# Re-ordered start, DMA transposes and new item weights in a planned adaLN block on one NeuronCore

## The chip, the cores and the metric

The kernel runs on one core of a Trainium2 chip. The metric is the device time of one launch in microseconds, taken as the median over runs. One more execution was taken by the hardware profiler, and all durations below come from that one.

## The reference

The input `x` has 2048 tokens of width 448. A condition row `c` gives six modulation rows by `silu(c) @ w_mod`. The block is an attention part and an MLP part, each behind a layer norm with modulation and each with a gated residual:

```python
sa, ca, ga, sb, cb, gb = (silu(c) @ w_mod) split in six
h = layernorm(x) * (1 + ca) + sa
x = x + ga * A(h)          # A: 16 heads of 28, each query sees 8 keys, 2 tokens apart; then @ wo
h = layernorm(x) * (1 + cb) + sb
x = x + gb * B(h)          # B: gelu(layernorm(h) @ w1 + b1) @ w2 + b2, inner width 1792
```

## The kernel before

**Tiling.** The tokens are held in two halves, the even tokens and then the odd ones, so that a window with steps of 2 becomes 8 neighbours within a half. There are 16 blocks of 128 tokens (`x_all`), and four chunks of 4 blocks. Attention runs in 17 groups (g0 to g16) of 121 queries against 128 keys.

**Stages.** The *front end* of a chunk takes the statistics of x (line 372), the power -1/2 on GpSimd (392), the normalised rows `z` in a `zbuf` (397), the transposes by TensorE into the PSUM tile `ptr` (482), and the modulation out of PSUM into `hT` (490 on ScalarE, 493 on VectorE). The projections to q and k follow (`pq`, 504), and their copies into `qT` and `kT` (360, 362). Chunk 0 is split into two front ends of two blocks, `front_end(0, 2, "x0")` and `front_end(2, 2, "x2")`; the others, of four blocks, begin at blocks 4, 8 and 12. *Attention* of a group is the logits `lt` (581), two exponentials `ex` (592), the mask `mk` (601), the values `pv` (616), `po` (626), the division `rd` and `on` (633, 637), a transpose `pt` (647) and its copy into `oT`. Per block follow the output projection `wo` (668) and the residual `x1` (673). The *second norm* (372 to 397, 692) ends in a `ybuf`, which a DMA issued by SyncE transposes into `yT` (707). The *MLP* of a chunk is `w1` (723) in 7 items of 8 matmuls, `ge`, the gelu (730), and per block `w2` (752), 14 matmuls. The term gb*b2 enters as one more matmul per block, ones-like `share` against the rows `gbb2_rows` (750). `fin` (762) adds the residual on VectorE, and SyncE stores the block (768).

**What sets the order.** Every step is an item of a `Plan` with the engines that it may run on and its duration on each. `Plan.order` simulates them once, at build time: among the items that are ready it picks the one with the earliest start, and among equal starts the longest remaining path, `tail`. `PRI` adds a weight to the tail of all items of a kind. Items are then emitted in the order of their simulated starts, so each engine's instruction order is fixed. `LANDS` gives the plan a time at which each load is there. `PHASES = [10, 17, 17, 17]` says how many attention groups come ahead of each chunk's MLP: the logits after a phase stand behind the last `w1` item of the MLP before, and its exponentials behind the last gelu. `SLOTS` counts the PSUM and SBUF buffers of each kind; `ptr`, `lt` and the output `p1` of w1 share the two buffers of the kind `lt`.

**The start.** SyncE issues the loads of c, of the first third of `w_mod` (`wmod`, columns sa and ca), of k, q and v weights and of the rest; ScalarE issues the loads x0 and x2. GpSimd clears pads and makes `ident` and `mask1`, VectorE copies `mask1` into `mask_rest` (560) and `silu_bf` into `silu_bc` (450). `idle(n)` issues n matmuls on zeros that nothing reads. 32 matmuls of one column (`ps_col`, 429) turn the modulation rows sa and ca into columns, which `mod1` (435 to 438) takes out of PSUM.

The key by which the plan before picks an item is

```python
key = (s, -tail[i], i)
```

Of the kernel before, what the change touches and what calls it, by code (L numbers as in the profile page):

```python
# [16 lines left out]
KT = 4  # L17
# [15 lines left out]
PHASES = [10, 17, 17, 17]  # L33
W2S = [(0, 5), (5, 10), (10, 14)]
SLOTS = {"lt": 2, "s": 3, "p2": 1, "et": 2, "on": 2, "vb": 3, "z2": 2, "yT": 2, "hm": 2, "xp": 4}

LANDS = [("c", 3.0), ("x0", 4.0), ("x2", 4.6), ("wmod", 7.8), ("wk", 8.6), ("wq", 9.4), ("wv", 10.3), ("x4", 12.5),
         ("wmod2", 18.0), ("wo", 19.5), ("b2", 20.5), ("x8", 22.0), ("w1", 28.0), ("w2", 33.0)]
NIDLE = 14
PLANS = None  # L40

PRI = {"po": -68.5, "r3": 10.0, "ve": -28.0, "lt": 6.0, "on": -24.0, "w2": -9.0, "ex": -20.0, "zt": 7.0,
       "r2": 53.3, "ge": -12.0, "w1": -13.0, "yt": 4.0, "y": 6.0, "z2": -7.0, "ml": -1.7, "pb": -5.0, "ot": 3.7,
       "pt": -0.6, "rd": 1.1, "h": 7.0, "mk": -2.0}
STATS_ACT = 2.0
XP = "PE"
# [5 lines left out]
class Plan:  # L52
# [8 lines left out]
    def add(self, name, eng, needs=(), after=(), uses=(), allocs=(), lag=0.09, tab=None, at=0.0, fn=None, pri=0.0):  # L61

        i = len(self.ops)
        self.index[name] = i
        self.ops.append(dict(name=name, eng=eng, needs=list(needs), after=list(after), allocs=list(allocs), lag=lag,
                             tab=tab, at=at, fn=fn, pri=pri + PRI.get(re.match(r"[a-z]+([0-9](?=_))?", name)[0], 0.0)))
        for b in list(uses) + list(allocs):
            self.bufs[b][1].append(i)

    def order(self, hop=0.07, table=1.3, win=3.413):  # L70
# [44 lines left out]
        while ready:  # L115
            best = None
            for i in ready:
                o = ops[i]
                t = o["at"]
                for j in o["need_i"]:  # L120
                    same = ops[j]["ran"] in o["eng"] and len(o["eng"]) == 1
                    t = max(t, end[j] + (0.0 if same else hop))
                for j in o["after_i"]:
                    t = max(t, start[j])
                ok, cntt = True, {}
                for b in o["allocs"]:
                    tg = tag_of[b]
                    st = slot_time(tg, cntt.get(tg, 0))
                    cntt[tg] = cntt.get(tg, 0) + 1
                    if st is None:  # L130
                        ok = False
                        break
                    t = max(t, st)
                if not ok:
                    continue
                fin = {e: max(t, free[e]) + d for e, d in o["eng"].items()}
                e = min(fin, key=lambda e: (fin[e], e))
                s = max(t, free[e])
                if o["tab"] and tab not in (None, o["tab"]):
                    s += table  # L140
                key = (s, -tail[i], i)
                if best is None or key < best[0]:
                    best = (key, i, e, s)
# [33 lines left out]
def kernel(  # L177
# [55 lines left out]
    NX1P = 4  # L233
    if XP == "PE":

        share = cst.tile([128, 128], BF16, name="share")
        gbb2_rows = cst.tile([128, D], BF16, name="gbb2_rows")
    else:
        x1p_ring = cst.tile([128, NX1P, D], FP32, name="x1p_ring")
# [18 lines left out]
    NZB = 3  # L258
# [17 lines left out]
    nc.sync.dma_start(out=c_row[:], in_=c)  # L276
    nc.scalar.dma_start(out=x_all[:, 0:2, :], in_=xv[:, 0, 0:2, :])
    nc.scalar.dma_start(out=x_all[:, 2:4, :], in_=xv[:, 0, 2:4, :])
    WM1 = 2 * D
    wmod = stp.tile([128, KT, WM1], BF16, name="wmod")  # L280
    load_ktiles(nc.sync, wmod, w_mod[:, 0:WM1], 0)
    wqk_st = stp.tile([128, KT, 2 * D], BF16, name="wqk_st")
# [19 lines left out]
    idle(4)  # L302
    for zb in zbufs:
        nc.vector.memset(zb[:, D:DP], 0.0)
    nc.gpsimd.memset(neg_half[:], -0.5)
# [5 lines left out]
    nc.gpsimd.memset(Wqk[64:128, KT - 1, :, :], 0.0)  # L311
# [3 lines left out]
    nc.gpsimd.memset(Wv[64:128, KT - 1, :], 0.0)  # L315
# [5 lines left out]
    nc.gpsimd.memset(wo_s[0:ZR_N, KT - 1, :], 0.0)  # L321
# [17 lines left out]
    if XP == "PE":  # L339
        nc.gpsimd.memset(share[:], 1.0 / 64)  # L340
# [7 lines left out]
    nc.gpsimd.memset(w1_s[64:128, KT - 1, :], 0.0)  # L348
# [74 lines left out]
    def col_fn(e):  # L423
        ps_col = T["ps_col"] = ps_s.tile([128, 2 * KT], FP32, name="ps_col", tag="s")
        for v in range(2):
            for j in range(KT):
                nj = kr_of(j)
                for kt in range(KT):
                    nc.tensor.matmul(ps_col[0:nj, v * KT + j:v * KT + j + 1],
                                     lhsT=wmod[0:kr_of(kt), kt, v * D + j * 128:v * D + j * 128 + nj],  # L430
                                     rhs=silu_bf[0:kr_of(kt), kt:kt + 1], start=(kt == 0), stop=(kt == KT - 1))
# [15 lines left out]
    P.add("idle", {"PE": 3.0}, after=["ps_c"], fn=lambda e: idle(NIDLE), pri=50.0)  # L447
    P.add("ps_col", {"PE": 1.3}, needs=["silu", "wmod"], after=["idle"], allocs=["ps_col"], lag=0.2, fn=col_fn)
    P.add("mod1", {"DVE": 0.3}, needs=["ps_col"], uses=["ps_col"], fn=mod1_fn)
    P.add("silu_bc", {"DVE": 0.33}, needs=["silu"], fn=lambda e: nc.vector.tensor_copy(  # L450
# [13 lines left out]
    def front_end(b0, nb, x_at):  # L464
        f = ("fe", b0)
        P.buf(f"ptr{b0}", "lt")
        for i in range(nb):
            stats(f"fst{b0 + i}", f, nb, i, lambda b=b0 + i: x_all[:, b, :], needs=[x_at])
        rstd(f"frs{b0}", f, nb, needs=[f"agfst{b0 + i}" for i in range(nb)])
        for i in range(nb):  # L470
# [6 lines left out]
            zs[zi] = b  # L477
            def t_fn(e, b=b, i=i, zi=zi):
# [8 lines left out]
        for kt in range(KT):  # L487
            def h_fn(e, kt=kt):
                if e == "ACT":
                    nc.scalar.activation(out=hT[:, kt, c0:c0 + w], in_=T["ptr", b0][:, kt, 0:w], func=ACT.Identity,  # L490
                                         bias=sa_col[:, kt:kt + 1], scale=ca1_col[:, kt:kt + 1])
                else:
                    nc.vector.tensor_scalar(out=hT[:, kt, c0:c0 + w], in0=T["ptr", b0][:, kt, 0:w],  # L493
                                            scalar1=ca1_col[:, kt:kt + 1], scalar2=sa_col[:, kt:kt + 1],
                                            op0=ALU.mult, op1=ALU.add)
            P.add(f"h{b0}.{kt}", {"ACT": 0.25 + 0.00084 * w, "DVE": 0.19 + 0.00053 * w},
                  needs=[f"zt{b0 + i}" for i in range(nb)] + ["mod1"], uses=[f"ptr{b0}"], fn=h_fn)
# [21 lines left out]
    for c4 in range(1, NCH):  # L519
        front_end(4 * c4, 4, "x4" if c4 == 1 else "x8")  # L520
# [20 lines left out]
    def use_gb(e, pb):  # L541
        nc.vector.tensor_copy(out=gb_bc[:], in_=pb[:])
        if XP == "PE":
            nc.vector.tensor_tensor(out=gbb2_rows[:], in0=pb[:], in1=b2_bc[:], op=ALU.mult)
            nc.vector.tensor_tensor(out=gbb2_bc[64:128, :], in0=pb[64:128, :], in1=b2_bc[64:128, :], op=ALU.mult)
            nc.vector.tensor_tensor(out=gbb2_rows[64:128, :], in0=gbb2_bc[64:128, :], in1=gbb2_rows[64:128, :],
                                    op=ALU.subtract)
        else:
            nc.vector.tensor_tensor(out=gbb2_bc[:], in0=pb[:], in1=b2_bc[:], op=ALU.mult)
# [10 lines left out]
    P.add("mask", {"DVE": 0.65}, fn=lambda e: nc.vector.tensor_copy(  # L560
# [151 lines left out]
    def mlp_items(c, gelu_after, w1_after):  # L712
# [23 lines left out]
        for bi, b in enumerate(bs):  # L736
            P.buf(f"p2_{b}", "s" if last and bi >= SLOTS["p2"] else "p2")
            if XP == "DVE":
                P.buf(f"xp{b}", "xp")
                def x_fn(e, b=b):  # L740
                    nc.vector.tensor_tensor(out=x1p_ring[:, b % NX1P, :], in0=x1_blk(b), in1=gbb2_bc[:], op=ALU.add)
                P.add(f"xp{b}", {"DVE": 0.53}, needs=[f"x1_{b}", "pb_gbe"], allocs=[f"xp{b}"],
                      after=[f"xp{b - 1}"] if b else [], fn=x_fn)
            for q in range(FT // 2):
                def fn(e, b=b, bi=bi, q=q):
                    if q == 0:
                        pool = ps_s if P.bufs[f"p2_{b}"][0] == "s" else ps_p2
                        T["p2", b] = pool.tile([128, D], FP32, name="p2", tag=P.bufs[f"p2_{b}"][0])
                        if XP == "PE":
                            nc.tensor.matmul(T["p2", b][:], lhsT=share[:], rhs=gbb2_rows[:], start=True, stop=False)  # L750
                    for ft in (2 * q, 2 * q + 1):
                        nc.tensor.matmul(T["p2", b][:], lhsT=T["hm", c][:, ft, bi * 128:(bi + 1) * 128],  # L752
                                         rhs=w2_s[:, ft, :], start=(ft == 0 and XP != "PE"), stop=(ft == FT - 1))
                kw = dict(uses=[f"hm{c}", f"p2_{b}"]) if q else dict(uses=[f"hm{c}"], allocs=[f"p2_{b}"])
                ws = [f"w2s{i}" for i, (f0, f1) in enumerate(W2S) if f0 < 2 * q + 2 and f1 > 2 * q]
                if XP == "PE" and q == 0:
                    ws = ws + ["pb_gbe"]
                P.add(f"w2_{b}.{q}", {"PE": (3 if XP == "PE" and q == 0 else 2) * 448 / 2400 + 0.005},
                      needs=[f"ge{c}.{q}"] + ws, lag=0.17, fn=fn,
                      after=[f"w2_{b}.{q - 1}"] if q else [], **kw)  # L760
            def f_fn(e, b=b):
                nc.vector.tensor_tensor(out=x_all[:, b, :], in0=T["p2", b][:], in1=x1_blk(b) if XP == "PE" else x1p_ring[:, b % NX1P, :],  # L762
                                        op=ALU.add)
            P.add(f"fin{b}", {"DVE": 0.54}, needs=[f"w2_{b}.{FT // 2 - 1}"] + ([f"xp{b}"] if XP != "PE" else []),
                  uses=[f"p2_{b}"] + ([f"xp{b}"] if XP != "PE" else []),
                  fn=f_fn)
# [22 lines left out]
    open_items = {P.index[n] for n in ("ps_col", "silu", "c_col", "wk0", "wk1", "wq0", "wq1", "ps_c", "idle")}  # L789
# [41 lines left out]
```

## Time and profile before

| What | Value |
|---|---|
| Median of 3 runs | 199.88 us (199.66 to 200.58) |
| The profiled execution's own time | 199.31 us |
| Its span, first to last instruction | 197.6 us |
| TensorE busy | 184.9 us, 1488 matmuls |
| VectorE, ScalarE, GpSimd busy | 129.8, 104.4, 24.8 us |
| Mean granted TensorE clock | 0.98 |
| Moved by DMA | 13.36 MB, nearly all in the first 30 us |

The span is what the instructions cover; the time of the execution is 1.7 us longer. A busy TensorE counts a matmul from its start to its modelled end, and matmuls overlap, so the pitch of a long run of them says more than their duration.

### The profile page before, as it was taken

How to read it: one execution, taken by the hardware profiler on the slowest of the kernel's cores; microseconds unless marked ns; L12 is line 12 of the kernel's file. 1: busy time of each engine (PE TensorE's matmuls, PEld its weight loads, DVE VectorE, ACT ScalarE, POOL GpSimd, SP SyncE). 2: the span in 40 equal slices, each digit the busy share in tenths (PEclk: the TensorE clock that was granted, in tenths of full speed). 3: DMA queues.
4: the chain of work that ended last, by engine and by line, in shares of the span. 5: the costliest groups of instructions: out<-in, count | busy, mean ns of one | idle time of the engine just before them, and what ended most of it. 6: DMA issues, size and time to landing. Idle time of an engine off the chain costs nothing.

```text
span 197.6 us, 3714 instructions
## 1 busy us (share of the span) xinstructions
PE 184.9 (94%) x1488; PEld 98.1 (50%) x1502; DVE 129.8 (66%) x325; ACT 104.4 (53%) x146; POOL 24.8 (13%) x57
## 2 busy tenths in 40 slices
PE   7949969989899999999989999999999999999993
PEld 2537745556454554545445555544444445444451
DVE  1877689989798799899879999899711011120021
ACT  3434879683888788465858665744224620204420
POOL 8732001100010201102000101211200000000000
PEclk9975999999999999999999999999999999999998
DMA  5999990000002020000230000015240000000002
GB/s 186 314 388 325 347 299 8 0 0 5 0 3 53 0 52 6 3 0 0 53 79 24 3 23 3 2 27 105 61 95 23 0 23 27 23 23 25 0 3 93
DMA packets 18454, 13.36 MB, mean 68 GB/s; under 512 B 9282, under 2 KB 17539, under 8 KB 18436
## 3 DMA queue, kind: packets, MB, share of 16 engines
q1 hardware_dynamic: 17892, 12.66, 22.1%
q10 hardware_dynamic: 544, 0.46, 0.8%
q8 instruction: 12, 0.20, 0.4%
q14 instruction: 6, 0.05, 0.1%
HBM read 9.18 MB, written 1.84 MB: 56 GB/s over the span
## 4 chain that ended last, share of the span: by engine, by line
PE 71%; DVE 17%; POOL 4%; ACT 3%; issue 3%; DMA 1%; POOLq 0%
PE p L752 20%; PE p L723 17%; PE pq L504 14%; PE pv L616 5%; PE pw L668 4%; DVE st L372 3%; ACT hT L490 3%; PE lt L581 2%; PE po L626 2%; DVE hT L493 2%; PE pt L647 2%; PE p L750 2%; POOL rs L392 2%; DVE x_all L673 2%; PE ptr L482 1%
## 5 line engine op out<-in xcount | busy, mean ns | idle before, releaser
L730 ACT ACTIVATE hm<-p 128x1024 bf16<-128x1024 f32 x28 | 28.6, 1024 | 52.1 <-PE p L723 51.0
L723 PE MATMUL p<-yT,w_s 128*128 128x512 bf16 x215 | 51.0, 379 | 0.6 <-DMA yT<-ybuf 0.2
L752 PE MATMUL p<-w_s,hm 128*128 128x448 bf16 x224 | 47.1, 352 | 0.0
L762 DVE TENSOR_TENSOR x_all<-p,x_all 128x448 bf16<-128x448 f32 x16 | 9.8, 620 | 46.0 <-PE p L752 46.0
L592 ACT ACTIVATE et<-lt 128x1024 bf16<-128x1024 f32 x34 | 33.7, 1030 | 5.5 <-PE lt L581 5.5
L723 PEld LDWEIGHTS <-w_s 128*128 128x128 bf16 x224 | 21.5, 98 | 24.9 <-issue 0.8
L504 PE MATMUL pq<-hT,Wqk 128*128 128x512 bf16 (+1 forms) x155 | 31.8, 355 | 0.9 <-DVE hT L493 0.5
L392 POOL TENSOR_TENSOR rs<-tv,neg_half 128x2 f32<-128x2 f32 (+1 forms) x21 | 17.1, 818 | 116.5 <-DVE tv L389 115.4
L752 PEld LDWEIGHTS <-hm 128*128 128x128 bf16 x224 | 21.3, 98 | 20.3 <-issue 1.0
L504 PEld LDWEIGHTS <-Wqk 128*128 128x128 bf16 x160 | 16.0, 105 | 12.3 <-issue 0.8
L601 DVE TENSOR_TENSOR et<-et,mask_rest 128x2048 bf16<-128x2048 bf16 x17 | 20.5, 1207 | 0.1
L372 DVE BATCH_NORM_STATS2 st<-x_all 128x6 f32<-128x448 bf16 x31 | 18.3, 609 | 0.1
L616 PE MATMUL pv<-Wv,hT 128*128 128x448 bf16 x68 | 15.3, 353 | 0.3 <-ACT kT L362 0.3
L668 PE MATMUL pw<-wo_s,oT 128*128 128x448 bf16 x64 | 14.6, 353 | 0.1
L362 ACT CAST vbuf<-pv 128x448 bf16<-128x448 f32 x15 | 8.1, 538 | 7.3 <-PE pv L616 7.2
L362 ACT CAST qT<-pq 128x512 bf16<-128x512 f32 (+1 forms) x19 | 9.5, 509 | 3.1 <-PE pq L504 2.8
L673 DVE TENSOR_TENSOR x_all<-pw,x_all 128x448 bf16<-128x448 f32 x16 | 9.9, 619 | 1.8 <-PE pw L668 1.8
L626 PEld LDWEIGHTS <-et 128*128 128x128 bf16 x272 | 9.0, 96 | 3.2 <-DVE vbuf L360 0.8
L637 DVE TENSOR_TENSOR on<-po,rden 128x448 bf16<-128x448 f32 x17 | 10.4, 614 | 0.1
L362 ACT CAST kT<-pq 128x512 bf16<-128x512 f32 (+1 forms) x17 | 8.5, 504 | 3.3 <-PE pq L504 3.0
L626 PE MATMUL po<-vbuf,et 128*128 128x29 bf16 x272 | 9.3, 176 | 0.5 <-DVE vbuf L360 0.5
L490 ACT ACTIVATE hT<-ptr,sa_col,ca_col 128x512 bf16<-128x512 bf16 (+1 forms) x10 | 6.7, 716 | 5.5 <-DVE hT L493 4.7
(99 smaller groups left out, 170.1 us busy)
## 6 DMA issues: line engine op xcount, KB each, us to landing
out_dram<-x_all SPq DMA_DIRECT2D x16, 112.0 KB, 1.7
w_s<-in_B_w_dram SPq DMA_DIRECT2D x1, 1568.0 KB, 13.9
wmod<-in_w_mod_dram SPq DMA_DIRECT2D x1, 1344.0 KB
w_s<-in_B_w_dram SPq DMA_DIRECT2D x1, 1344.0 KB, 14.9
x_all<-in_A_x_dram SPq DMA_DIRECT2D x1, 896.0 KB
wmod<-in_w_mod_dram SPq DMA_DIRECT2D x1, 672.0 KB, 5.3
wqk_st<-in_A_wqkv_dram SPq DMA_DIRECT2D x2, 336.0 KB, 5.8
x_all<-in_A_x_dram ACTq DMA_DIRECT2D x2, 224.0 KB, 4.1
```

The lines of the kernel that those rows point to most:

```text
L362: nc.scalar.copy(out=out, in_=in_)
L372: nc.vector.bn_stats(out=st[:], in_=src())
L392: nc.gpsimd.tensor_tensor(out=rs[:], in0=T["tv", tile_key][:], in1=neg_half[:, 0:n], op=ALU.pow)
L504: nc.tensor.matmul(pq[:, 0:w], lhsT=Wqk[:, kt, m, :], rhs=hT[:, kt, c0:c0 + w], start=(kt == 0), stop=(kt == KT - 1))
L592: nc.scalar.activation(out=et_v[:, 2 * half:2 * half + 2], in_=T["lt", g][half][:].rearrange("p r (ft c) -> p r ft c", ft=4), func=ACT.Exp ...
L601: nc.vector.tensor_tensor(out=et[:], in0=et[:], in1=mask_rest[:], op=ALU.mult)
L616: nc.tensor.matmul(pv[:], lhsT=hT[:, kt, k0:k0 + BK], rhs=Wv[:, kt, :], start=(kt == 0), stop=(kt == KT - 1))
L626: nc.tensor.matmul(po[:, h, :], lhsT=T["et", g][:, h, :], rhs=vbufs[g % NVB][:, h, :], start=True, stop=True)
L668: nc.tensor.matmul(pw[:], lhsT=oT[:, kt, jb * 128:(jb + 1) * 128], rhs=wo_s[:, kt, :], start=(kt == 0), stop=(kt == KT - 1))
L723: nc.tensor.matmul(p1[:, f, 0:w], lhsT=w1_s[:, kt, ft * 128:(ft + 1) * 128], rhs=T["yT", c][:, kt, 0:w], start=(kt == 0), stop=(kt == KT - 1))
L730: nc.scalar.activation(out=T["hm", c][:, 2 * q:2 * q + 2, 0:w], in_=T["p1", c, q][:, :, 0:w], func=ACT.Gelu_apprx_tanh)
L752: nc.tensor.matmul(T["p2", b][:], lhsT=T["hm", c][:, ft, bi * 128:(bi + 1) * 128], rhs=w2_s[:, ft, :], start=(ft == 0 and XP != "PE"), sto ...
```

## The change

- **Loads.** `wmod` is split into the columns sa (on SyncE's queue) and ca (on ScalarE's queue, behind x0 and ahead of x2). The plan gets their times as `wmsa` and `wmca`.
- **Start.** Four clears move from GpSimd to VectorE. `silu_bc` and `mask` may not start in the plan before 10.0 us (`later`). `ps_col` becomes two items, `ps_sa` and `ps_ca`. 11 idle matmuls stand where 14 stood, and 4 more after `ps_ca` and `zt1`. The statistics of blocks 2 and 3 stand behind `frs0a`.
- **Transposes.** For the chunks at blocks 8 and 12 (`Z_DMA`), `z` is transposed by a DMA of SyncE straight into `hT`, and the modulation runs in place in `hT`, on VectorE alone. A fourth `zbuf` is added.
- **gb*b2.** The extra matmul stays for blocks 0 to 3 and 15 (`XPE`). For the other 11, `fin` is two additions on VectorE, the first with `gbb2_bc` into an fp32 tile `xt`.
- **Order.** `PHASES` becomes `[9, 14, 17, 17]`. The key weighs the tail against the start (`LOOK`), `PRI` has new values, and `NUDGE` adds weights to about 140 single items.

```diff
-PHASES = [10, 17, 17, 17]
+PHASES = [9, 14, 17, 17]
...
-LANDS = [("c", 3.0), ("x0", 4.0), ("x2", 4.6), ("wmod", 7.8), ("wk", 8.6), ("wq", 9.4), ("wv", 10.3), ("x4", 12.5),
-         ("wmod2", 18.0), ("wo", 19.5), ("b2", 20.5), ("x8", 22.0), ("w1", 28.0), ("w2", 33.0)]
-NIDLE = 14
+LANDS = [("c", 3.0), ("x0", 5.0), ("x2", 5.8), ("wmsa", 6.4), ("wmca", 7.2), ("wk", 8.4), ("wq", 9.4), ("later", 10.0),
+         ("wv", 10.4), ("x4", 12.5), ("wmod2", 18.0), ("wo", 19.5), ("b2", 20.5), ("x8", 22.0), ("w1", 28.0),
+         ("w2", 33.0)]
+NIDLE = [11, 4]
+LOOK = 0.000121
+PRI = {"ad": -181.5, "agfst": -82.1, "ags2": -347.3, "ex": -137.9, "ge": -154.4, "h": -94.5, "lt": 209.3,
...
+NUDGE = {"ad12": 15.6, "ad2": -30.3, "ad8": 44.8, "agfst12": -48.8, "agfst6": 98.9, "ags2_13": -79.7,
...
-XP = "PE"
+Z_DMA = (2, 3)
+XPE = (0, 1, 2, 3, 15)
...
-                key = (s, -tail[i], i)
+                key = (s - LOOK * tail[i], -tail[i], i)
...
     nc.scalar.dma_start(out=x_all[:, 0:2, :], in_=xv[:, 0, 0:2, :])
+    load_ktiles(nc.sync, wmod[:, :, 0, :], w_mod[:, 0:D], 0)
+    load_ktiles(nc.scalar, wmod[:, :, 1, :], w_mod[:, D:2 * D], 0)
     nc.scalar.dma_start(out=x_all[:, 2:4, :], in_=xv[:, 0, 2:4, :])
-    load_ktiles(nc.sync, wmod, w_mod[:, 0:WM1], 0)
...
+    nc.vector.memset(Wqk[64:128, KT - 1, :, :], 0.0)
     for zb in zbufs:
         nc.vector.memset(zb[:, D:DP], 0.0)
+    nc.vector.memset(Wv[64:128, KT - 1, :], 0.0)
+    nc.vector.memset(wo_s[0:ZR_N, KT - 1, :], 0.0)
+    nc.vector.memset(w1_s[64:128, KT - 1, :], 0.0)
...
-    P.add("idle", {"PE": 3.0}, after=["ps_c"], fn=lambda e: idle(NIDLE), pri=50.0)
+    P.add("idle", {"PE": 2.4}, after=["ps_c"], fn=lambda e: idle(NIDLE[0]), pri=50.0)
+    P.add("ps_sa", {"PE": 1.05}, needs=["silu", "wmsa"], after=["idle"], allocs=["ps_col"], lag=0.2,
+          fn=lambda e: col_fn(0), pri=20.0)
+    P.add("ps_ca", {"PE": 1.05}, needs=["ps_sa", "wmca"], uses=["ps_col"], lag=0.2, fn=lambda e: col_fn(1), pri=20.0)
+    P.add("idle2", {"PE": 0.213 * NIDLE[1]}, after=["ps_ca", "zt1"], fn=lambda e: idle(NIDLE[1]), pri=50.0)
...
+            if by_dma:
+                P.add(f"zt{b}", {"SP": 1.25}, needs=[f"z{b}"], after=[f"zt{b - 1}"] if i else [], lag=1.2,
+                      fn=lambda e, b=b, zi=zi: nc.sync.dma_start_transpose(
+                          out=hT[:, :, tok_col(b):tok_col(b) + 128], in_=zbufs[zi % NZB][:]))
+                continue
...
+                src = hT[:, kt, c0:c0 + w] if by_dma else T["ptr", b0][:, kt, 0:w]
...
-                        if XP == "PE":
+                        if b in XPE:
                             nc.tensor.matmul(T["p2", b][:], lhsT=share[:], rhs=gbb2_rows[:], start=True, stop=False)
...
+                if b not in XPE:
+                    xt = wk.tile([128, D], FP32, name="xt", tag="xt")
+                    nc.vector.tensor_tensor(out=xt[:], in0=src, in1=gbb2_bc[:], op=ALU.add)
+                    src = xt[:]
+                nc.vector.tensor_tensor(out=x_all[:, b, :], in0=src, in1=x1_blk(b), op=ALU.add)
```

## The prediction, made before the change was run

> **What bounds the kernel now.** I read the page first, for the busiest engine and the chain that ended last.
>
> ```profile
> span 197.6 us, 3714 instructions
> ...
> PE 184.9 (94%) x1488; PEld 98.1 (50%) x1502; DVE 129.8 (66%) x325; ACT 104.4 (53%) x146; POOL 24.8 (13%) x57
> ...
> PE   7949969989899999999989999999999999999993
> PEld 2537745556454554545445555544444445444451
> DVE  1877689989798799899879999899711011120021
> ...
> PE 71%; DVE 17%; POOL 4%; ACT 3%; issue 3%; DMA 1%; POOLq 0%
> ```
>
> TensorE (PE) carries 71% of the chain. VectorE (DVE) is full only until slice 28 (138 us); behind that it is nearly idle while PE is full. A matmul that goes is worth its pitch; a VectorE addition behind 138 us is worth nothing.
>
> Next the busy times by stretch (busy time and count of PE, PEld, DVE, ACT, POOL; then granted PE clock, DMA share, GB/s).
>
> ```profile
> 5.00:10.00 5.00, 4.77 (x43) 2.87 (x41) 4.35 (x14) 2.29 (x9) 3.58 (x15) 1.00 1.11 316
> 10.00:15.00 5.00, 2.42 (x20) 1.52 (x20) 3.71 (x18) 1.82 (x5) 1.49 (x2) 0.71 1.07 388
> 15.00:20.00 5.00, 5.00 (x30) 3.73 (x29) 3.84 (x15) 2.46 (x8) 1.01 (x1) 0.60 1.09 328
> ```
>
> Here is PE's hole: half idle from 10 to 15 us, then on a lowered clock. The same view by single microseconds puts the half clock at 12 to 19 us. The timeline shows why work starts so late:
>
> ```profile
> 5.58 0.95 DVE L560 COPY mask_rest<-mask 128x2048 bf16<-128x2048 bf16 x1 [3.99 <-POOL mask L325]
> ...
> 7.50 0.16 DVE L421 TENSOR_TENSOR silu_bf<-e_c,c_col 128x4 bf16<-128x4 f32 x1
> ...
> 8.12 1.10 DVE L450 COPY silu_bc<-silu_bf 128x512 bf16<-128x512 bf16 x1
> ...
> 14.75 6.46 PE L504 MATMUL pq<-hT,Wqk 128*128 128x256 bf16 x39 [0.54 <-DVE hT L493]
> ```
>
> VectorE stood 4 us at `mask_rest` for a mask that GpSimd had not made; the columns of c, ready for it at 3.6 us, were queued behind, then the statistics of x0. Projections run without a break from 14.75 us.
>
> Last the chain of waits, for PE's pitch (start, length) in the PE-bound stage:
>
> ```profile
> 186.32 1.14 PE p L752 x6
> 187.46 1.73 PE p L723 x8
> ...
> 190.32 0.19 PE p L750
> ```
>
> So 0.19 us for a matmul of 448 columns, 0.216 for 512. From rows of the chain: w1 28 x 1.73, w2 and its bias 240 x 0.19, wide `pq` 96 x 0.216, narrow `pq` 64 x 0.118, `pv`, `pw` and modulation rows 37 x 0.76, `po` 17 x 0.39, `lt` 17 x 0.34, `pt` 17 x 0.22, `ptr` 16 x 0.23: 170 us. Of that all but 1 us lies between 14.75 and 194.3, or 179.6 us. Only 10 to 11 us there are not PE at full pitch.
>
> **The change part by part**, against the profiled execution (199.31 us: span 197.6 and 1.7 around it).
>
> *Start.* Four clears come to VectorE, ahead of the columns of c: as 32-bit words 512, 224, 224 and 896 a row, at 0.27 us for the 256 of `idle_in` 1.9 us. VectorE is free at 1.7, so about 3.7 us, near the 3.6 at which c is there. From c's column to `silu_bf` took 6.45 to 7.66, so 5.0 us now. The sa and ca columns take half of 2.25 us each. `wmod` landed 5.3 us after its issue at 1.20, at 6.5; the idle matmuls end about 0.65 earlier than at 7.58, at 6.9. So `ps_sa` and `ps_ca` end near 9.1, `mod1` near 9.5; the four narrow `hT` (0.40 on VectorE, 0.56 on ScalarE, shared out) near 10.7. The key weights landed 5.8 us after 2.29, in time. The deferred copies (0.95 and 1.10) still have to run, beside PE's projections. First row: 14.75 to 10.7, **-4.0**; bounds 0 and -5.
>
> A second queue could speed up loading: the first row has the DMA engines' share at 1.11 already, so I credit none. The Trainium skill (DMA: Bandwidth & Descriptors, "Issuing engines are not separate DMA queues") says that queues of several issuing engines share the same 16 DMA engines and save only issue time; that speaks against "two queues" as such, and by it, too, this term would be nothing. The order of loads does change: x2 stood second on ScalarE's queue and now has 392 KB ahead of it, at 316 GB/s some 1.3 us. Its statistics stand behind x0's, and the 32 projections of x0 (3.5 us) cover it.
>
> *Clock.* 39 narrow projections took 6.46 us, 0.166 each, where the twelve after them took 1.42, 0.118 each. With the clock kept up **-1.9**; bounds 0 and -1.9. The clock fell at 12.1, after 4.5 us of one-column matmuls, transposes and gaps. Now only 6.9 to 9.1 is such work, with 4 idle matmuls (0.9 us) behind it, so I take the whole.
>
> The Trainium skill (TensorE: Matmul & The Clock Gate, Part 1) has the clock halved after an idle window of about 3.4 us; no idle stretch of PE in the timeline there is longer than 1.25. Its Part 4 says that transposes don't count as busy in the same way, and that would fit. By Part 1 alone this term would have to be 0, since no gap was long enough; the sum would be 1.9 us higher.
>
> *gb\*b2.* 11 matmuls leave PE, all in stages where PE is full: 11 x 0.19 = **-2.1**. 11 additions of 0.62 us (line 762's mean) come to VectorE: 6.8 us. The blocks concerned are 4 to 14, finished mostly behind 138 us beside an idle VectorE: 0. Without that cover the additions of blocks 4 to 7 would stand ahead of norm and mask work: up to +2.5. At the end blocks 12 to 14 finish together: VectorE did three additions from 191.30, now six at 0.56, until 194.7, and block 15's, ready at 194.33, stands behind them: **+0.4**.
>
> *Transposes.* Two chunks of four blocks lose 32 PE transposes:
>
> ```profile
> 48.54 0.46 PE ptr L482 x8
> ```
>
> 4 x 0.46 = **-1.8**, on the chain here. ScalarE and VectorE lose eight PSUM reads of 0.78 and 0.54; VectorE gains eight in-place ones near line 397's 0.38. That is even for VectorE, and 3 us less for ScalarE. SyncE gains 8 issues; a like one is
>
> ```profile
> L707 SPq DMA_TRANSPOSE yT<-ybuf x16: 1191/1213/2201, 59.0 to 145.0; - x16
> ...
> DMA to landing us min/median/max: 2.4/2.5/4.1
> ```
>
> so four in a row land 3 x 1.2 + 2.5 = 6.1 us after the first z where PE took 0.5 a pair. SyncE has nothing else to issue from 17 to 59 us. PE meanwhile has projections, values and modulation rows of the chunk before (PE is busy 9.95 of the 10 us from 30 to 40), so 0; bare, it is 5 us a chunk, +10.
>
> The logits wait for `ptr`'s readers because they share two PSUM buffers:
>
> ```profile
> PE lt L581 <- DVE hT L493: 1.7, 2, 1.1
> ```
>
> Of these, 1.1 us is chunk 4's and stays; the other, at 51.7, goes: **-0.6**.
>
> *Chunk 4.* Its x lands at 7.01 + 5.1 = 12.1 us as before, while PE comes 6 us earlier. From statistics to `hT` the chain needs 2.2 + 0.4 + 1.0 + 1.4 + 0.4 + 1.8, so about 19 us at best; PE has 64 x 0.118 and some transposes from 10.7, until about 18.7. ScalarE and VectorE are loaded in that stretch: **+1.0**, bounds 0 and +2.2.
>
> *Order.* `PHASES` 9, 14, 17 makes two more changes of ScalarE's table, 1.28 us each, on an engine with 53% busy. The boundary of before (66 to 90 us) cost PE 1 us of idle. Against that the second MLP now fills PE between groups 13 and 16. I cannot tell the new weights' order from the trace: **0**, with all the rest of PE's loss (about 5 us) as the one bound and the rivals as the other.
>
> Sum: -4.0 -1.9 -2.1 +0.4 -1.8 -0.6 +1.0 = -9.0, so 199.31 becomes 190.3. The runs' median stands 0.57 above the profiled execution, so 190.9.
>
> **The rivals.** *The early start is given back* (B). VectorE is at 90% or more from 30 to 138 us, and if its queue sets the pace there, the 5.9 us of start and clock shrink or vanish: 190.9 + 3.1 to + 5.9, 194 to 196.8. For it: PE itself waits for VectorE in the list of waits, at `zbuf`, `hT` and `x_all`. Against: its waits there sum to a few microseconds, and at 138 us PE still has 10 us of chunk 1's w2 in reserve.
>
> *The new order fills PE's holes* (C): of the 10 to 11 us, 1.9 is the clock and 3 to 4 is the start and chunk 4; the remaining 5 would give 186 to 188. For it: PE loses least where w2 runs between the groups (100 to 120 us).
>
> *The DMA transposes sit bare* (D, slower). Place: PE's in-order queue at the first projection of chunks 2 and 3. Price: 6.1 less the 1.2 that PE and the copies take now, about 5 us a chunk, plus the logits queued behind the projections and everything on ScalarE and VectorE behind those. Twice 5 only eats the 9.0; it decides from a bare wait of 5 us a chunk, and at 7 (a transpose landing at 4.1 and the loads until 30 us in the same queue) the time is 190.9 + 14 = 205. Against: work of the chunk before is there. The phase boundaries would add to it, but not alone: group 13's logits come at 106.9, after the last transposed block of chunk 1 at 104.6.
>
> *It does not do what it says*: the clock falls all the same, because `zt1` comes late. That is +1.9 and lies inside the range.
>
> **How the numbers follow.** Forecast (188 to 193): 0.60. B: 0.21, of which 0.17 shows. C: 0.10. D and its like: 0.09. A measurement of this kernel can tell 0.5% from no change, 1.0 us: faster than 198.9 is 0.87, within 0.04, slower 0.09. The range from 186.0 to 197.3 takes in B and C and leaves out D.
>
> **What would show it.** Right: projections in a run from about 10.7 us on clock 1.00 up to 20 us; 5 matmuls of gb*b2; 32 `ptr` matmuls and no wait of `lt` for `hT` of chunk 3; VectorE busier by 5 to 8 us behind 100 us and PE still full there; the last store a little behind block 15's w2. Wrong: first projections after 13 us; PE waiting on `hT<-zbuf` DMAs; PE less than nine tenths busy in more slices between 30 and 140 us than now.

## The result and the profile after

The changed kernel takes 190.46 us in the median of 4 runs (190.26 to 190.64), the kernel before 200.06 us (199.66 to 200.58). The ratio is 0.952, 95% interval 0.949 to 0.954. The prediction said 190.9 us. By the medians the fall is 9.6 us, by the two profiled executions 8.8; the profiled one of before lies 0.75 us under its median. The profiled execution of after took 190.52 us, its span is 188.8, so the 1.7 us around the span are as before.

The page of after, its busy times, three rows of slices and the chain:

```profile
span 188.8 us, 3664 instructions
...
PE 179.8 (95%) x1446; PEld 94.5 (50%) x1460; DVE 140.3 (74%) x344; ACT 105.4 (56%) x149; POOL 23.7 (13%) x53
...
PE   7989899899999898999999999999999999999993
...
DVE  5688799996998999967989998399999602202451
...
PEclk9969999999999999999999999999999999999999
...
PE 72%; DVE 15%; DMA 5%; POOL 2%; issue 2%; ACT 1%; ACTq 1%; DVEq 0%
PE p L755 25%; PE p L778 23%; PE pw L700 6%; DVE st L396 5%; PE pv L648 4%; PE pq L539 4%; DMA x_all<-in_A_x_dram 3%; PE lt L613 2%; PE pt L679 2%; POOL rs L416 2%; PE po L658 2%; DMA yT<-ybuf 2%; PE ptr L517 1%; DVE hT L529 1%; DVE zbuf L421 1%
```

The bound is the same: TensorE carries 72% of the chain (71% before). VectorE has 10.5 us more work; behind 100 us it is 6.4 more (46.5 to 52.9), most of it in slices where it stood nearly idle before. What is new in the chain is "DMA 5%" (1% before): by the page's row of lines, 3% is a load of x and 2% the transposes into `yT`. The start shows the load. The windows of the first stage, with the same columns as in the prediction:

```profile
5.00:10.00 5.00, 4.66 (x42) 2.89 (x41) 3.48 (x13) 0.00 (x0) 0.71 (x1) 0.98 1.09 300
10.00:15.00 5.00, 4.78 (x35) 3.43 (x36) 4.37 (x21) 2.89 (x7) 1.70 (x1) 0.68 1.06 387
15.00:20.00 5.00, 5.00 (x58) 4.09 (x57) 4.07 (x14) 4.49 (x11) 1.38 (x1) 1.00 1.09 293
...
9.00:10.00 1.00, 0.66 (x10) 0.53 (x10) 1.00 (x5) 0.00 (x0) 0.00 (x0) 0.88 1.10 304
10.00:11.00 1.00, 1.00 (x9) 0.83 (x9) 1.00 (x8) 0.00 (x0) 0.65 (x1) 0.50 1.12 319
...
13.00:14.00 1.00, 1.00 (x13) 0.93 (x11) 0.56 (x2) 0.52 (x2) 0.00 (x0) 0.91 1.01 401
```

PE's hole from 10 to 15 us is filled, until 13.3 us with transposes and idle matmuls. The clock still falls in that window (to a half from 9.8 to 13.2 us, by the rows of single microseconds), but it is full again from 15 to 20 us, where it was 0.60. The timeline of after, the rows that decide the first projection:

```profile
8.31 1.15 DVE L396 BATCH_NORM_STATS2 st<-x_all 128x6 f32<-128x448 bf16 x2 [1.45 <-DMA x_all<-in_A_x_dram]
9.46 0.36 DVE L421 TENSOR_SCALAR zbuf<-x_all,mv,rs 128x448 bf16<-128x448 bf16 x1
...
11.12 0.14 DVE L462 COPY sa_col<-ps_col 64x1 f32<-64x1 f32 x1
...
12.54 0.90 PE L517 MATMUL ptr<-ident,zbuf 128*128 128x128 bf16 x8
13.28 4.97 PE L539 MATMUL pq<-hT,Wqk 128*128 128x256 bf16 x44
```

The first unbroken projections are at 13.28 us, not at 10.7. VectorE stood 1.45 us until x2 had landed, and the normalised rows of x0, whose statistics were long there, stood behind x2's statistics in its queue.

**The account**, profiled execution against profiled execution (span -8.8 us):

| Stretch | Before | After | Difference | Forecast |
|---|---|---|---|---|
| start of span to first unbroken projection | 14.75 | 13.28 | -1.5 | -4.0 |
| from there to the end of the last matmul | 179.6 | 172.4 | -7.2 | -5.4 |
| behind the last matmul | 3.3 | 3.2 | -0.1 | +0.4 |

In the second row, 11 matmuls at 0.19 and 32 transposes at 0.0575 make -3.9 us of work that is gone, as forecast. The other -3.3 is PE's loss (10.4 us before, 7.1 after). The clock has about 1.9 of it; 1.4 are other holes, where the forecast had +0.4 (chunk 4 +1.0, the logits -0.6). So the sum came out right with one term 2.5 us too large and others 2.3 too small in all. That they cancel is luck. The experiments take this apart.

### The profile page after: what moved, and what is told of

It is laid out like the page before. It is cut to its first block, busy times and chain, and to the rows that moved or that the text cites. A ratio compares the mean times of both kernels' runs of the same rounds, so it can differ in the third digit from the quotient of the medians.

```text
span 188.8 us, 3664 instructions
## 1 busy us (share of the span) xinstructions
PE 179.8 (95%) x1446; PEld 94.5 (50%) x1460; DVE 140.3 (74%) x344; ACT 105.4 (56%) x149; POOL 23.7 (13%) x53
## 4 chain that ended last, share of the span: by engine, by line
PE 72%; DVE 15%; DMA 5%; POOL 2%; issue 2%; ACT 1%; ACTq 1%; DVEq 0%
PE p L755 25%; PE p L778 23%; PE pw L700 6%; DVE st L396 5%; PE pv L648 4%; PE pq L539 4%; DMA x_all<-in_A_x_dram 3%; PE lt L613 2%; PE pt L679 2%; POOL rs L416 2%; PE po L658 2%; DMA yT<-ybuf 2%; PE ptr L517 1%; DVE hT L529 1%; DVE zbuf L421 1%
## 5 line engine op out<-in xcount | busy, mean ns | idle before, releaser
L778 PE MATMUL p<-w_s,hm 128*128 128x448 bf16 x224 | 48.3, 352 | 0.1
L416 POOL TENSOR_TENSOR rs<-tv,neg_half 128x2 f32<-128x2 f32 (+1 forms) x21 | 20.0, 954 | 125.1 <-DVE tv L413 102.5
L539 PE MATMUL pq<-hT,Wqk 128*128 128x512 bf16 (+1 forms) x155 | 29.2, 335 | 0.8 <-DVE qT L384 0.6
L791 DVE TENSOR_TENSOR xt<-p,gbb_bc 128x448 f32<-128x448 f32 x11 | 6.8, 622 | 27.0 <-PE p L778 26.9
L539 PEld LDWEIGHTS <-Wqk 128*128 128x128 bf16 x160 | 15.3, 98 | 12.0 <-issue 1.1
L396 DVE BATCH_NORM_STATS2 st<-x_all 128x6 f32<-128x448 bf16 x30 | 17.8, 615 | 1.6 <-DMA x_all<-in_A_x_dram 1.4
L386 ACT CAST kT<-pq 128x512 bf16<-128x512 f32 (+1 forms) x19 | 9.6, 508 | 4.6 <-PE pq L539 4.1
L669 DVE TENSOR_TENSOR on<-po,rden 128x448 bf16<-128x448 f32 x17 | 10.5, 619 | 0.1
L396 DVE BATCH_NORM_STATS2 st<-z 128x6 f32<-128x448 bf16 x16 | 9.2, 615 | 0.1
```

The lines of the kernel that those rows point to most:

```text
L386: nc.scalar.copy(out=out, in_=in_)
L396: nc.vector.bn_stats(out=st[:], in_=src())
L416: nc.gpsimd.tensor_tensor(out=rs[:], in0=T["tv", tile_key][:], in1=neg_half[:, 0:n], op=ALU.pow)
L539: nc.tensor.matmul(pq[:, 0:w], lhsT=Wqk[:, kt, m, :], rhs=hT[:, kt, c0:c0 + w], start=(kt == 0), stop=(kt == KT - 1))
```

## The experiments

All runs below use stand-ins: each `dma_start_transpose` is replaced by a plain DMA of the same bytes between the same tiles, so the MLP, and in the changed structure also two chunks of `hT`, work on untransposed data. Nothing else differs. In outline:

```diff
-nc.sync.dma_start_transpose(out=X, in_=buf[:])
+nc.sync.dma_start(out=X, in_=buf[:].rearrange("p (k n) -> p k n", k=KT))
```

16 such copies run in *copy before* and 24 in *copy after*. Every other kernel is *copy after* with one edit, unless it is said otherwise. Each was timed in five rounds. "First projection" is the first row of the unbroken run of `pq` in the timeline.

| Kernel | Time, us | Ratio to before, 95% | First projection |
|---|---|---|---|
| copy before | 199.49 | 1.001 (0.998 to 1.003) | 14.74 |
| copy after | 189.88 | 0.951 (0.948 to 0.953) | 12.96 |
| x2 ahead of the ca columns | 188.77 | 0.946 (0.942 to 0.949) | 12.07 |
| ca columns on SyncE's queue | 188.29 | 0.945 (0.943 to 0.948) | 11.51 |
| 9 more idle matmuls | 191.14 | 0.958 (0.954 to 0.962) | 13.89 |
| 12 idle matmuls fewer | 190.67 | 0.957 (0.955 to 0.959) | 13.48 |
| mask and `silu_bc` not deferred | 189.21 | 0.949 (0.947 to 0.951) | 12.96 |
| gb*b2 by TensorE in all 16 blocks | 192.08 | 0.962 (0.958 to 0.965) | 13.35 |
| z transposed by TensorE everywhere | 196.27 | 0.981 (0.976 to 0.986) | 12.93 |
| old weights and old phases | 194.46 | 0.974 (0.970 to 0.978) | 14.14 |
| old weights, new phases | 207.43 | 1.042 (1.039 to 1.045) | 14.47 |
| copy before, new weights and phases | 206.59 | 1.034 (1.030 to 1.038) | 14.37 |

In the last three kernels one to four single projections run ahead of that row, from 12.69, 12.44 and 13.77 us, with breaks behind them.

### Are the DMA transposes on the path? (copy before, copy after)

> The kernel before, with its 16 DMA transposes of ybuf replaced by plain DMAs of the same bytes (the blocks arrive untransposed, so the data of the MLP is not the reference's). It is a yardstick for the next ones. A plain store of a block lands 1.7 us after its issue where the transpose took 2.5, and takes 0.35 us of SyncE where the transpose took 1.2. If no transpose's latency is on the path but the 2.71 us stretch at 135.9, the time is 199 to 200; if several are, 197 or less.

> The changed kernel with its 24 DMA transposes (8 of zbuf, 16 of ybuf) replaced by plain DMAs of the same bytes, order unchanged (untransposed data). If the 8 new transposes are hidden behind the chunk before, as forecast, it takes 190.46 less at most 0.7 (the one wait for yT in the list): 189.7 to 190.5. If they sit bare, the shorter latency (about 0.8 us a landing and 0.85 us of SyncE each, 3.4 a chunk of four) shows: 187 or less.

The stand-ins have the ratios of the originals within the intervals (1.001 for 1, 0.951 for 0.952). What a DMA transpose costs beyond a plain DMA of the same size is thus not on the path in either kernel. That is mostly the time on SyncE's queue, 0.59 us for a plain one against 1.2. From issue to landing the plain one takes 2.3 us, the transpose 2.4, so the 1.7 us that the expectation took from the stores was too low, and these runs don't tell whether the landing itself is on the path. In after itself the eight new ones lie here:

```profile
L509 SPq DMA_TRANSPOSE hT<-zbuf x8: 1190/1217/1309, 31.8 to 44.6; - x8
L529 DVE TENSOR_SCALAR hT<-hT,ca_col,sa_col x8: 327/406/416, 38.3 to 51.1; 128x512 bf16<-128x512 bf16 x8
```

These are the rows of the tile `hT` (min, median, max in ns, then first and last start). From the first issue at 31.8 to the first modulation at 38.3 there are 6.5 us; the prediction had 6.1 until the fourth lands. VectorE has no idle time ahead of that first modulation, so the transposes landed by then at the latest. TensorE does not feel them: its list of waits has no entry for a DMA into `hT`, nor for `hT`'s modulation.

### Does an earlier start reach the end? (x2 first, one queue, start late)

```diff
# x2 ahead of the ca columns
 load_ktiles(nc.sync, wmod[:, :, 0, :], w_mod[:, 0:D], 0)
+nc.scalar.dma_start(out=x_all[:, 2:4, :], in_=xv[:, 0, 2:4, :])
 load_ktiles(nc.scalar, wmod[:, :, 1, :], w_mod[:, D:2 * D], 0)
-nc.scalar.dma_start(out=x_all[:, 2:4, :], in_=xv[:, 0, 2:4, :])
# ca columns on SyncE's queue
-load_ktiles(nc.scalar, wmod[:, :, 1, :], w_mod[:, D:2 * D], 0)
+load_ktiles(nc.sync, wmod[:, :, 1, :], w_mod[:, D:2 * D], 0)
# 9 more idle matmuls, in idle2
-fn=lambda e: idle(NIDLE[1])
+fn=lambda e: idle(NIDLE[1] + 9)
```

> copy_after with the load of x2 ahead of the ca columns on ScalarE's queue; instruction order on PE, VectorE and GpSimd unchanged. Theory: the start was held by x2, which landed at 8.28 and held VectorE, and with it z0 and z1, and PE, which has the transposes of blocks 2 and 3 ahead of the first projection; with x2 at about 6.9 the first projection comes at 12.0 instead of 13.28, and since PE is the bound behind it, the time falls 1.2 below copy_after. Rival, given back further on (VectorE or chunk 4's load at 12.4 sets the pace): first projection at 12.0 and at most 0.3 us gained. Rival, the key and query weights hold the start: first projection at 13, time unchanged.

> copy_after (189.9) with both halves of the first third of w_mod on SyncE's queue (sa, then ca, then the key weights), x0 and x2 alone on ScalarE's queue; orders of PE, VectorE and GpSimd unchanged. Theory: the second queue bought no bandwidth and only put 392 KB ahead of x2; with x2 landing near 6.7, as before the change, the first projection comes at 12 and the time is 188.8, as with x2 first. Rival, two queues load faster in sum: key weights and ca columns land 0.5 us later and the first projection stays at 13: 190.

> copy_after with 9 more idle matmuls between zt1 and zt2 (9 x 0.216 = 1.9 us on a full clock, up to 3.8 on a half clock; PE waited 0.3 us for z2 there). Theory, PE is the bound from the first projection on: the first projection moves by 1.6 to 3.5 us and the end by the same. Rival, slack further on: the end moves by less than half of what the first projection moves.

Profiled executions, all on a mean clock of 0.999 or 1.000, against copy after's 189.44 us:

| Edit | First projection moved | Time moved |
|---|---|---|
| x2 first | -0.89 | -0.75 |
| ca columns on SyncE's queue | -1.45 | -1.58 |
| 9 more idle matmuls | +0.93 | +0.95 |

The medians move by -1.11, -1.59 and +1.26 us; in the last of the three kernels three of six executions are on a clock of 0.991. The 9 idle matmuls moved the first projection by 0.93 us and not by the 1.6 or more that was expected: in copy after TensorE stood 1.02 us ahead of the transposes of blocks 2 and 3 as it was. The start goes through to the end nearly one for one, in both directions. This is against rival B, by which VectorE sets the pace and the start is given back. The timeline of the kernel with the ca columns on SyncE's queue:

```profile
6.64 1.15 DVE L396 BATCH_NORM_STATS2 st<-x_all 128x6 f32<-128x448 bf16 x2
...
10.52 0.69 DVE L421 TENSOR_SCALAR zbuf<-x_all,mv,rs 128x448 bf16<-128x448 bf16 x2
...
11.51 4.75 PE L538 MATMUL pq<-hT,Wqk 128*128 128x256 bf16 x42
```

x2's statistics begin at 6.64 with no wait ahead of them, 1.67 us before those in after, and the projections follow. The loads of `wmod` on the other queue cost this kernel nothing: `ps_col` ran from 6.52 there, from 6.82 in copy after and 7.28 in after. So putting the ca columns ahead of x2 on the second queue lost about 1.6 us. With x2 first the ca columns come later in turn: `ps_col` waits 0.75 us for them in two places, and less is gained.

### Are the deferrals and the idle matmuls worth anything? (not deferred, no idle)

```diff
# not deferred: only the emitted order is edited
+for name, ahead_of in (("mask", "c_col"), ("silu_bc", "agfst0")):
+    todo.remove(P.index[name])
+    todo.insert(todo.index(P.index[ahead_of]), P.index[name])
# no idle: 2 and 1 idle matmuls run where 11 and 4 ran
-idle(NIDLE[0]) ... idle(NIDLE[1])
+idle(2) ... idle(1)
```

> copy_after with the copies into mask_rest and silu_bc put back to where the kernel before has them in VectorE's order (ahead of c's columns, and behind x0's statistics); the rest unchanged. My term of the start took 2 us for their leaving. If they were on the path, the first projection moves from 12.96 by about 1 to 2 us and the time to 191 or 192. Rival: GpSimd's mask is now there at 3.4 us and x2 at 8.3 holds VectorE anyway, so both hide in that wait and the two copies leave the later, fuller stretch: 189.0 to 189.9.

> copy_after with 12 of the 15 idle matmuls behind ps_c left out, order otherwise unchanged. Theory: PE then does nothing but one-column matmuls and transposes from 3.5 us to the first projection, the clock is at half there and stays so for one to two windows of 3.4 us, each costing half its length: 1.7 to 3.4 us more, 191.6 to 193.3. Rival, copies out of PSUM set the pace of the narrow projections and PE's clock there is worth less than 0.8: up to 190.7.

With the mask and `silu_bc` back at their early places the first projection is at 12.96 as in copy after, and the time is no longer (189.21 against 189.88). Both copies fit in VectorE's wait for x2. With that wait gone, as in the one-queue version, the deferral could matter; it was not tried there.

The idle matmuls are less clear. Windows of the profile with 12 fewer:

```profile
5.00:10.00 5.00, 2.44 (x33) 2.08 (x33) 3.37 (x13) 0.00 (x0) 0.71 (x1) 0.79 1.08 314
10.00:15.00 5.00, 3.81 (x25) 2.73 (x26) 4.25 (x22) 2.41 (x5) 1.70 (x1) 0.50 1.07 390
15.00:20.00 5.00, 5.00 (x33) 3.84 (x32) 4.07 (x14) 2.73 (x8) 1.38 (x1) 0.69 1.09 315
```

In this execution (191.34 us) the clock was at a half from 7.9 to 18.1 us. Its projections begin 0.5 us later than copy after's and its end comes 1.9 us later, so 1.4 us were lost behind the start, where 44 projections took 7.23 us for copy after's 4.97. But three of the other four executions of the same kernel, 190.25 to 190.67 us, show a mean clock of 1.00. So the forecast of 191.6 to 193.3, by which the clock is always lost there, missed. The median lies in its rival's range, up to 190.7. Whether the rival's reason holds, a clock worth less than 0.8 us there, is not settled: the execution with the half clock is 0.7 to 1.1 us above those three. Those three are still 0.4 to 1.2 us above copy after's three on a clock of 1.00; why is open. The clock fell or not by execution, with the same instructions. Nor did after itself always lose it: its four runs have mean clocks of 0.991, 0.989, 1.000 and 1.000, and the times go along: 190.52, 190.64, 190.40, 190.26.

### What is gb*b2 worth? (bias all PE)

```diff
-if b in XPE:
+if b in XPE_RUN:      # range(16); also in the start flag and in fin
```

> copy_after (189.9) with gb*b2 as a matmul for all 16 blocks; each engine's order otherwise unchanged, since the plan keeps its durations. If PE is the bound wherever blocks 4 to 14 are finished and the second additions were free, 11 matmuls of 0.19 us come back: 192.0. If the additions cost something on the path, their going gives some of it back: below 191.4.

The order stays as it is; only 11 matmuls come back and 11 additions go. By the medians it costs 2.2 us, by the ratios 2.1 (0.0107 x 199.5). Four of its five executions are on a clock of 0.991; the one on 0.999 took 191.56, 1.7 to 2.1 us above copy after's on 1.00. The forecast was 11 x 0.19 = 2.1. In after, the tile `xt`:

```profile
L791 DVE TENSOR_TENSOR xt<-p,gbb_bc x11: 614/624/625, 122.7 to 182.8; 128x448 f32<-128x448 f32 x11
```

The first of the additions is at 122.7 us and nobody is listed as waiting for them. At the end, which was to cost 0.4 us:

```profile
182.83 0.62 DVE L791 TENSOR_TENSOR xt<-p,gbb_bc 128x448 f32<-128x448 f32 x1 [1.36 <-PE p L778]
183.49 0.62 DVE L793 TENSOR_TENSOR x_all<-xt,x_all 128x448 bf16<-128x448 f32 x1
185.67 0.62 DVE L793 TENSOR_TENSOR x_all<-p,x_all 128x448 bf16<-128x448 f32 x1 [1.55 <-PE p L778]
```

Block 15's addition waits for its own matmuls (they end at 185.64), with VectorE idle for 1.55 us before. Blocks 12 to 14 no longer finish together ahead of it, because the new order spreads them.

### What are the TensorE transposes worth? (z by PE)

```diff
-Z_DMA = (2, 3)
+Z_DMA = ()
```

> copy_after with the chunks at blocks 8 and 12 transposed by PE through PSUM again (the plan is made anew around it, with the same weights). By my terms 1.8 us of PE and 0.6 us of logits waiting for PSUM come back: 192.3. Rival, the weights were fitted to the DMA transposes and the new plan loses more: 193.5 or more. Rival, the DMA path cost as much as it saved: 190.

Executions on a mean clock of 0.999 or 1.000 took 194.36 and 194.59 us, those on 0.982 to 0.988 took 196.2 to 196.6, and one on 0.971 197.93. Against copy after's median of 189.88 the fastest of them is 4.5 us longer; the forecast gave 1.8 + 0.6 = 2.4, and the expectation's first rival, 193.5 or more, came true. TensorE's list of waits (us in total, times, longest):

```profile
PE lt L612 <- ACT hT L525: 1.7, 1, 1.7
PE lt L612 <- DVE hT L528: 1.5, 1, 1.5
```

Two logits wait 3.2 us for the modulation that reads `ptr`, because `lt` and `ptr` share PSUM buffers. Together with 32 transposes at 0.0575 that is 5.0. The prediction knew this wait from one group (0.6). The plan was made anew for this kernel with weights that had been set for the other structure, so how much of the 3.2 belongs to the transposes and how much to the order cannot be told.

### What are the new weights and phases worth? (old weights, weights alone, new phases)

```diff
# old weights and old phases, in the new structure
-PRI = {new}; NUDGE = {about 140 entries}; LOOK = 0.000121; PHASES = [9, 14, 17, 17]
+PRI = {old}; NUDGE = {};                  LOOK = 0.0;      PHASES = [10, 17, 17, 17]
# old weights, new phases: as above, but
+PHASES = [9, 14, 17, 17]
# weights alone: copy before with the new PRI, NUDGE, LOOK and PHASES
```

> copy_after's structure (loads, clears, split columns, zbuf by DMA, gb*b2 for 5 blocks) planned with the old weights, no single-item weights, no look-ahead and phases 10, 17, 17, 17. What my terms give to the structure (start 1.7, clock 1.9, gb*b2 2.1, transposes 1.8) stays and 1 to 2 us of the order go: 191 to 192.5. Rival, the order is most of the gain: 195 or more.

> copy_before (199.5) with only the new weights, the single-item weights, the look-ahead and phases 9, 14, 17, 17. If the order by itself is worth 1 to 2 us: 197.5 to 198.5. Rival, it is most of the gain: 195 or less. Rival, the weights serve only the structure they were made with: 199.5 or more.

> copy_after's structure with the old weights, no single-item weights, no look-ahead, but the new phases 9, 14, 17, 17 (the kernel with the old phases took 194.46). If moving the second MLP ahead of groups 14 to 16 is what fills PE: 191.5 to 193. Rival, the phases alone do nothing or cost the two table changes: 194 to 197, and the weights are the gain.

The structure alone (old weights and phases) gives 5.0 us: 199.49 to 194.46. That time is above the 191 to 192.5 expected and under the rival's 195. Weights and phases give another 4.6, to 189.88. Put on the old structure, the same weights and phases cost 7.1 us, and the phases without the weights cost 13.0 in the new structure, where the expectation and its rival had 197 at most. The weights are a property of the pair, not an improvement in themselves.

Where old weights lose: part of it is at the start, where the unbroken projections begin at 14.14 us against 12.96, though four come ahead of them (0.5 us of work). Another part is at the end. Their list of waits has

```profile
PE p L756 <- DVE xt L769: 1.4, 2, 0.7
```

which is w2 waiting for a PSUM buffer that the first of the two additions still holds, and from the last matmul to the end of the span there are 3.8 us instead of 3.2. So here the additions are not free: 2.0 us of the 5.0 by which the spans of the profiled executions differ. The rest was not taken apart.

Where new phases without the weights lose is mostly one place. Windows of copy after, then of the kernel with the phases alone:

```profile
40.00:50.00 10.00, 9.89 (x106) 5.10 (x106) 8.17 (x19) 7.71 (x13) 0.79 (x1) 1.00 0.07 16
50.00:60.00 10.00, 9.79 (x94) 5.00 (x85) 9.77 (x25) 8.39 (x13) 1.35 (x2) 1.00 0.01 2
```

```profile
40.00:50.00 10.00, 8.34 (x117) 4.77 (x115) 10.00 (x24) 6.62 (x9) 0.79 (x1) 0.99 0.03 8
50.00:60.00 10.00, 4.21 (x40) 1.77 (x39) 9.92 (x22) 2.82 (x4) 0.92 (x1) 0.50 0.14 31
```

PE busy falls from 9.79 to 4.21 us in the window from 50 to 60 while VectorE is full, and the clock halves on top. Against old weights with the old phases, PE is busy 7.2 us less from 40 to 60 us (12.55 for 19.78). The clock from 40 to 70 us costs an estimated 3.8 more (busy time times the part of the clock that is missing: 4.21 x 0.50 + 9.55 x 0.17 + 8.34 x 0.01). That is 11.0 of the 12.7 us by which the spans differ. The longest wait is

```profile
PE pq L517 <- DVE x_all L683: 3.6, 1, 3.6
```

that is, projections released only after a residual `x1` (line 683) on VectorE. On VectorE's queue, from 53.78 us until that residual, stand the rows of gb and gb*b2 (2.2 us), the modulation of four `hT` (1.4), two norms (0.7) and the first scaling of w2 by gb (1.1). So with the boundaries earlier VectorE has work for the first MLP ahead of what the projections of the next chunk wait for. That is read from this wait and the full VectorE. It was not tried by itself, and neither was one of the two boundaries (9 for 10, 14 for 17) without the other. With the new weights the same boundary leaves PE 9.79 of 10 us busy.

## Why the prediction was right, point by point

The total was right, in part by luck: errors of opposite sign cancelled. What was named as the bound held: TensorE, from the first projection to the end. Three runs that only shift the start show it. One of the signs that the prediction named for being wrong did come, first projections after 13 us (13.28). The others did not: no wait of TensorE for the DMAs into `hT`, and three slices between 30 and 140 us with PE under nine tenths, as before. Of the steps:

- **Start, -4.0: mis-sized, -1.5 measured.** The step that failed is "Its statistics stand behind x0's, and the 32 projections of x0 (3.5 us) cover it". x2's load did come later, as foreseen. But its statistics hold VectorE's in-order queue 1.45 us, with x0's `z` and `mod1` behind (columns out of PSUM by 11.26 instead of 9.5 us), and PE's own order has the transposes of blocks 2 and 3 ahead of the first projection. Moving the load gave 1.45 of the missing 2.5 us back. About 0.3 is the difference between after (13.28) and copy after (12.96), where the clock did not fall. For the last 0.8, from 10.7 to 11.51, the trace of the one-queue kernel shows what stood there: the normalised rows of blocks 2 and 3 come at 10.52, though GpSimd had finished what they need at 9.89. They stand behind eight copies of `Wqk` in VectorE's queue (1.6 us), which the prediction did not price. No run moved these copies.
- **No credit for the second queue: right in the sign of its doubt, still too kind.** The trace showed the DMA engines' share at 1.11 already, and one queue for all of `wmod` is 1.6 us faster than two in the changed kernel's arrangement.
- **Clock, -1.9: about that, but not for the reason given.** The clock did fall in the profiled execution of after, from 9.8 to 13.2 us. It cost little because the projections began when it was nearly over; before, the half clock lasted until 19 us. In two of four runs of after the mean clock was full.
- **gb\*b2, -2.1 and 0 for the additions: shown** (2.1 to 2.2 by the run with all 16 matmuls). **Tail, +0.4: 0**, by the order of the last blocks; under the old order the cost exists, at 0.6 and 1.4.
- **Transposes, -1.8 and 0 for the wait: the wait of TensorE for the DMAs is not there, as argued.** The term itself came out as a lower bound: together with the logits' wait for `ptr`'s readers (forecast 0.6) taking it back cost 4.5 us or more, an unknown part of it by the order. One reading was off beside the path: VectorE lost four reads of `ptr` (4 x 0.54 = 2.2 us) and got eight in place (8 x 0.41 = 3.2), so it is not even but about 1 us more.
- **Chunk 4, +1.0: not there.** In that stage TensorE waits 0.6 us once, from 20.0 us, for VectorE's copy into `qT`, and is idle 0.8 us from 20 to 30 us in all, where it had been idle 1.5 from 26 to 30 us before.
- **Order, 0: mis-sized.** In the new structure it is worth 4.6 us. The prediction had it as rival C with 0.10. It gave 9.0 us to the structure and 0 to the order; the stand-ins gave 5.0 and 4.6. The time landed on the forecast because the order's gain and the short start nearly cancel: with x2 landing early the same kernel stands at 188.3, near C's 186 to 188.
- **Rival D** had the wrong mechanism (the transposes) and played the boundary down ("The phase boundaries would add to it, but not alone"). The slower side was in the boundaries: without the weights they cost 13.0 us and give 207.4, about the 205 named for D.

## What to carry to other kernels

When PE is the bound, price the start by what stands in the *in-order queues* ahead of the first useful matmul, VectorE's and PE's: a load that lands late takes along all that is queued behind its first reader. Weights of a planned order can be right for one structure and cost several per cent on another, so read "0 for the order" as the widest term of the sum and let the range carry it. On this evidence, a load should go ahead of another on the same queue only if its reader, with what is queued behind it, is needed first.

The best version run here is the stand-in with the ca columns on SyncE's queue, 188.29 us. That same edit on the changed kernel itself was not run.

## What the runs showed of the hardware

- **The clock varies between executions of one kernel.** A single half-clock window in after lasted from 9.8 to 13.2 us, 3.4 us. The same kernels, run again, show a mean clock of 1.00 or 0.99. What it costs differs: 0.1 to 0.4 us between the four runs of after, in whose profile the projections began as the window ended, and 1.5 to 2.1 in the six runs with 9 more idle matmuls (190.11 to 190.39 against 191.90 to 192.16 us), where no profile shows the window's place. The Trainium skill (TensorE: Matmul & The Clock Gate, Part 1) has windows of about 3.4 us that run freely, so that the point at which the clock changes varies. The length agrees with these runs; that free-running windows are the reason for the variation is not shown here. By the same part the clock falls after an idle window. In after there was no idle stretch of TensorE near that length ahead of the fall, only 2.3 us of one-column matmuls and a gap of 0.2, so on that the measurement stands against it. What counts as idle was not settled: most executions with 12 idle matmuls fewer kept the full clock.
- **The modulation in place, bf16 in SBUF, takes VectorE 0.41 us for 128x512**, against 0.54 with PSUM as the source (the largest of `hT<-ptr` on VectorE in after).
- **A plain DMA of 128 KB within SBUF lands hardly sooner than a DMA transpose of the same bytes**: 2.3 us from issue to landing against 2.4 in the changed kernel. Its time on SyncE's queue is half, 0.59 against 1.2 us.
